# Attention start on one core: square sums split between two engines, softmax in halves, loads and conversion steps moved

## The chip, the cores and the metric

The kernel runs on one core of one Trainium2 chip. Its time is device microseconds of one execution; the number compared is the median over several runs. A profile is one further execution, taken by the hardware profiler. In what follows PE is TensorE (matmuls), PEld its weight loads, DVE is VectorE, ACT is ScalarE, POOL is GpSimd and SP is SyncE, which issues the DMAs. L12 is line 12 of the kernel.

## The reference

The attention runs over channels (256 x 256 scores, summed over 6016 tokens), then two dense blocks follow over the 6016 tokens.

```python
qn = q / (norm(q, axis=1) + 1e-6); kn = k / (norm(k, axis=1) + 1e-6)   # per channel, over tokens
s = kn.T @ qn / tau; a = softmax(s)            # 256 x 256
x = v @ a                                      # 6016 x 256
h = x @ w_in                                   # 256 -> 2048
g = where(h >= 1, h, where(h <= -1, 0, (h + 1)**2 / 4)); x = g @ w_out     # 2048 -> 256
xn = x / sqrt(mean(x*x) + 1e-6) * rms_g
out = (silu(xn @ w_gate) * (xn @ w_val)) @ w_out2                          # 256 -> 1536 -> 256
```

q, k, v and tau are float32. The five weight matrices come as float64.

## The kernel before, in words

**Start.** q and k come in 14 pieces of 2 to 4 rows per partition (`QK_CHUNKS`, 47 rows in all), one DMA each for q (L369) and k (L370), into 9 rotating tiles `qk`. For each piece ACT squares q and k (L379), DVE adds the squares into the four-row sum `acc` in SBUF (L381), and PE multiplies the raw k by the raw q: `scores(ci, b)` (L354) does the piece `ci` for the half `b` of the 256 score rows, one float32 matmul per row, which the profile shows as two matmul instructions of 256 columns each. Half 0 of a piece is written out when the piece comes, half 1 five pieces later (`BEHIND`). After the last piece DVE folds `acc` to one row (L387), PE sums it over the partitions into `n_ps` and `k_ps` (L409, L411), ACT takes the roots, DVE the reciprocals (L482 to L487), and the scaled scores go through the softmax (L491 to L497).

**First quarter of w1.** The kernel never forms v @ a: since x @ w_in = v @ (a @ w_in), it makes w1 = a @ w_in in four quarters of 512 columns, each for two halves of 128 rows. For `product_a(0)` (L441) PE first transposes both halves of the exponentials (L503), ACT and DVE split them into a high and a low part (`ah`, `al`, L126 and L123); then come 6 matmuls of 512 columns per half (L451), and ACT writes the high and DVE the low part of w1 (L460, L461). DVE and ACT work here in the order in which it is written (`in_order`).

**Float64 weights.** Each weight tile of 512 KB (`wide`, L195 and L197) is turned into a high and a low float32 part by `narrow` (L203): DVE clamps (L206), ACT or DVE takes the low word (L211, L213), DVE joins (L217, L225) and subtracts (L123), ACT takes the absolute value and the high part (L221, L231). This is cut into five steps; `pump()` (L271) takes each of up to two running jobs one step further and begins another. In the start three tiles of w_in are converted so (`PUMPS`); in the main loop there is one pump per block and another at every third. `gates` holds steps back behind given instructions.

**Main loop.** For each tile of 512 tokens and each of 16 slices of the 2048 columns, a block ("1", t, f) does six matmuls for h (`emit_A`, L553), ACT and DVE compute g (L570 to L572) and split it (L126, L123), and three blocks later six matmuls add to y (`emit_B`, L587). Tiles 0 and 1 are interleaved: (0,0), (0,1), (1,0), (0,2), ... The quarters 1 to 3 of w1 are made at blocks 5, 13 and 21 (`make_w1`). Blocks ("2", t, f) of the second dense block begin after 60 blocks of the first kind. h and the start's small products share four PSUM buffers (`mm_tile`).

**Order.** The instruction order of each engine is set ahead of time by a planner, from the order in which they are written, priorities (`AHEAD_OF`) and its own estimate of times; `in_order` fixes the written order for the engines it names. On the chip each engine works strictly through its list.

Of the kernel before, what the change touches and what calls it, by code (L numbers as in the profile page):

```python
# [34 lines left out]
BEHIND = 5  # L35
AHEAD = 3
# [13 lines left out]
def tile_channel_attention_two_ffn(  # L50
# [152 lines left out]
    def narrow(x, hi, lo, on_act):  # L203
# [26 lines left out]
        got = low.bitcast(F32)  # L230
        nc.scalar.activation(out=hi, in_=got, func=AF.Copy)  # L231
# [11 lines left out]
    def narrow_job():  # L243
        if not wide:
            fetch()
        key, x, dst = wide.pop(0)
        ahead = STAGE - FLIGHT
        if BORROW[0] <= n_wide[0] < BORROW[1]:
            ahead += LENT
        while jobs and n_wide[0] >= EARLY and len(wide) < ahead:  # L250
            fetch()
        hi, lo = dst()
        yield from narrow(x, hi, lo, key[0] != "wo")
        ready.add(key)
# [11 lines left out]
    may_W2 = [False]  # L266

# [3 lines left out]
    def pump():  # L271
        for job in flight[:]:
            if step_job(job) == "end":
                flight.remove(job)
        if len(flight) < FLIGHT and (wide or jobs) and (key_next() in FIRST or may_W2[0]):
            job = narrow_job()
            step_job(job)
            flight.append(job)

# [44 lines left out]
    for at_job, job in zip((1, 4, 5, 8, 9), late_wi):  # L324
        later.insert(at_job, job)
# [21 lines left out]
    acc = sp.tile([P, 2, JM, C], F32, name="acc")  # L347
# [16 lines left out]

    for ci, nj in enumerate(QK_CHUNKS):
# [19 lines left out]
        h = {NQ - 3: 2, NQ - 1: 1}.get(ci)  # L385
        if h:
            last_sum = nc.vector.tensor_tensor(  # L387
                out=acc[:, :, :h, :], in0=acc[:, :, :h, :], in1=acc[:, :, h:2 * h, :],
                op=ALU.add,
            )  # L390
        scores(ci, 0)
        if ci >= BEHIND:
            scores(ci - BEHIND, 1)
        if ci in FETCH_AT:
# [46 lines left out]
    def product_a(g):  # L441

        h, l = wi.pop(g)
        got = []
        for b in range(NC):
            ah, al = at[b]
            ps = mm_tile(f"w1_ps{g}_{b}")
            terms = [(ah, w, c) for c in range(NC) for w in (h, l)]
            terms += [(al, h, c) for c in range(NC)]
            for i, (x, w, c) in enumerate(terms):  # L450
                nc.tensor.matmul(  # L451
                    ps, x[:, c * P:(c + 1) * P], w[:, c, :],
                    start=(i == 0), stop=(i == len(terms) - 1),
                )
            got.append(ps)

        def evict(b):
            sl = slice(g * TOK, (g + 1) * TOK)
            hi, lo = w1h[:, b, sl], w1l[:, b, sl]
            nc.scalar.activation(out=hi, in_=got[b], func=AF.Copy, scale=rs[b])  # L460
            nc.vector.scalar_tensor_tensor(  # L461
                out=lo, in0=got[b], scalar=rs[b], in1=hi.bitcast(F32),
                op0=ALU.mult, op1=ALU.subtract,
            )
            if b == NC - 1:
                w1_made.add(g)
# [3 lines left out]
    ENG = mybir.EngineType  # L470
    with in_order(ENG.DVE, ENG.Activation):
        with tc.issue_after(last_sum.ins):
            for c in range(NC):
                turn_v(0, c)
        nc.scalar.activation(out=rq, in_=n_ps[:, :C], func=AF.Sqrt)
        nc.scalar.activation(
            out=rk, in_=k_ps[:, :2 * NC].rearrange("p (b x) -> p b x", x=2)[:, :, 0],
            func=AF.Sqrt,
        )

        nc.scalar.activation(out=seen, in_=ones[:, :1], func=AF.Exp)
        nc.vector.tensor_scalar(out=rq, in0=rq, scalar1=1e-6, scalar2=None, op0=ALU.add)  # L482
        nc.vector.reciprocal(out=rq, in_=rq)
        nc.vector.tensor_scalar(
            out=rk, in0=rk, scalar1=1e-6, scalar2=tau_sb, op0=ALU.add, op1=ALU.mult
        )
        nc.vector.reciprocal(out=rk, in_=rk)  # L487
        for c in range(NC):
            v_hi(0, c)
        for b in range(NC):  # L490
            nc.vector.scalar_tensor_tensor(  # L491
                out=s_sb[b], in0=s_ps[b], scalar=rk[:, b:b + 1], in1=rq,
                op0=ALU.mult, op1=ALU.mult,
            )
            nc.vector.tensor_reduce(out=mx[b], in_=s_sb[b], op=ALU.max, axis=AX.X, negate=True)

            nc.scalar.activation(  # L497
                out=s_sb[b], in_=s_sb[b], func=AF.Exp, bias=mx[b], accum_out=rs[b]
            )
        a_ps = [mm_tile(f"a_ps{b}")[:, :C] for b in range(NC)]  # L500
        for b in range(NC):
            for c in range(NC):
                nc.tensor.transpose(  # L503
                    a_ps[b][:, c * P:(c + 1) * P], s_sb[b][:, c * P:(c + 1) * P], ident
                )
        v_lo(0, 0)
        for b in range(NC):
            ah = atp.tile([P, C], F32R, name=f"ah{b}")
            al = atp.tile([P, C], F32R, name=f"al{b}")
            split(ah, al, a_ps[b])  # L510
            at.append((ah, al))
            nc.vector.tensor_scalar(
                out=rs[b], in0=rs[b], scalar1=1e-9, scalar2=None, op0=ALU.add
            )
            nc.vector.reciprocal(out=rs[b], in_=rs[b])
# [392 lines left out]
```

## Time and profile before

| | us |
|---|---|
| median of 3 runs | 1175.72 (1175.22 to 1175.86) |
| profiled execution | 1174.88 |
| its span in the trace | 1173.1 |
| PE busy in the span | 1156.6 (99%) |
| DVE busy | 661.6 (56%) |
| ACT busy | 642.2 (55%) |
| GpSimd busy | 69.6 (6%) |

The span is what the trace covers; 1.8 us of the execution lie around it. Busy shares are averages over the whole span. The page's slices of 29 us and the table by stretch show where an engine is full. A row of a timeline gives start, duration, engine, line, operation and tiles, and in brackets how long the engine had stood idle before it and what ended that.

### The profile page before, as it was taken

How to read it: one execution, taken by the hardware profiler on the slowest of the kernel's cores; microseconds unless marked ns; L12 is line 12 of the kernel's file. 1: busy time of each engine (PE TensorE's matmuls, PEld its weight loads, DVE VectorE, ACT ScalarE, POOL GpSimd, SP SyncE). 2: the span in 40 equal slices, each digit the busy share in tenths (PEclk: the TensorE clock that was granted, in tenths of full speed). 3: DMA queues.
4: the chain of work that ended last, by engine and by line, in shares of the span. 5: the costliest groups of instructions: out<-in, count | busy, mean ns of one | idle time of the engine just before them, and what ended most of it. 6: DMA issues, size and time to landing. Idle time of an engine off the chain costs nothing.

```text
span 1173.1 us, 14011 instructions
## 1 busy us (share of the span) xinstructions
PE 1156.6 (99%) x5202; PEld 966.7 (82%) x5202; DVE 661.6 (56%) x1034; ACT 642.2 (55%) x1092; POOL 69.6 (6%) x54
## 2 busy tenths in 40 slices
PE   8889999999999999999999999999999999999998
PEld 7768878888888888888888888888888888888898
DVE  5999999844554554553554454464454455553433
ACT  6688899755555545555554554554545454333332
POOL 0000000100100101101101100010010011010000
PEclk9999999999999999999999999999999999999999
DMA  9923344010020020010011001002001001010110
GB/s 351 233 107 100 98 116 118 1 19 1 1 36 1 1 36 1 1 28 9 1 18 18 1 12 25 1 1 32 1 1 18 1 1 19 1 18 1 19 18 14
DMA packets 107747, 43.36 MB, mean 37 GB/s; under 512 B 97568, under 2 KB 97952, under 8 KB 107680
## 3 DMA queue, kind: packets, MB, share of 16 engines
q1 hardware_dynamic: 107680, 42.48, 14.6%
q8 instruction: 40, 0.66, 0.2%
q14 instruction: 27, 0.22, 0.1%
HBM read 36.31 MB, written 6.16 MB: 36 GB/s over the span
## 4 chain that ended last, share of the span: by engine, by line
PE 87%; DVE 5%; DMA 3%; ACT 3%; SPq 1%; issue 1%; ACTq 0%; DVEq 0%
PE y L595 18%; PE h L561 18%; PE gp L675 16%; PE vp L675 16%; PE o L719 15%; DVE acc L381 1%; PE o L709 1%; DMA qk<-in_k_dram 1%; DMA wide<-in_moe_w_val_dram 1%; SPq L164 1%; DMA wide<-in_moe_w_out_dram 1%; DVE g L572 1%; ACT g L570 1%; DMA qk<-in_q_dram 1%; ACT gh L126 1%
## 5 line engine op out<-in xcount | busy, mean ns | idle before, releaser
L572 DVE SCALAR_TENSOR_TENSOR g<-h,g 128x512 f32<-128x512 f32 (+1 forms) x192 | 129.9, 677 | 157.3 <-ACT g L571 157.1
L126 ACT ACTIVATE uh<-u 128x512 fp32r<-128x512 f32 (+1 forms) x144 | 89.8, 623 | 206.2 <-PE o L719 170.7
L686 DVE TENSOR_TENSOR u<-u,vp 128x512 f32<-128x512 f32 (+1 forms) x144 | 97.2, 675 | 159.5 <-PE vp L675 156.9
L570 ACT ACTIVATE g<-h 128x512 f32<-128x512 f32 (+1 forms) x192 | 111.9, 586 | 115.6 <-PE h L561 112.6
L126 ACT ACTIVATE gh<-g 128x512 fp32r<-128x512 f32 (+1 forms) x192 | 119.0, 621 | 82.6 <-DVE g L572 82.1
L561 PE MATMUL h<-vh,w1h 128*128 128x512 f32 (+1 forms) x384 | 148.8, 388 | 2.2 <-DVE g L572 2.2
L123 DVE TENSOR_TENSOR ul<-u,uh 128x512 fp32r<-128x512 f32 (+1 forms) x144 | 97.6, 678 | 92.0 <-ACT uh L126 85.4
L561 PE MATMUL h<-vl,w1h 128*128 128x512 f32 (+1 forms) x384 | 148.8, 388 | 0.0
L595 PE MATMUL y<-gh,woh 128*128 128x512 f32 (+1 forms) x384 | 148.0, 385 | 0.8 <-ACT gh L126 0.6
L595 PE MATMUL y<-gh,wol 128*128 128x512 f32 (+1 forms) x384 | 147.7, 385 | 0.0
L123 DVE TENSOR_TENSOR gl<-g,gh 128x512 fp32r<-128x512 f32 (+1 forms) x168 | 113.6, 678 | 56.0 <-ACT gh L126 54.7
L685 ACT ACTIVATE u<-gp 128x512 f32<-128x512 f32 (+1 forms) x144 | 84.8, 589 | 79.7 <-PE gp L675 66.6
L571 ACT ACTIVATE g<-g 128x512 f32<-128x512 f32 (+1 forms) x192 | 118.6, 622 | 4.5
L561 PE MATMUL h<-vh,w1l 128*128 128x512 f32 (+1 forms) x384 | 117.9, 387 | 0.0
L595 PE MATMUL y<-gl,woh 128*128 128x512 f32 (+1 forms) x384 | 117.0, 386 | 0.7 <-DVE gl L123 0.7
L675 PE MATMUL gp<-xh,wgl 128*128 128x512 f32 (+1 forms) x288 | 111.0, 385 | 0.0
L675 PE MATMUL gp<-xh,wgh 128*128 128x512 f32 (+1 forms) x288 | 111.0, 385 | 0.0
L675 PE MATMUL vp<-xh,wvl 128*128 128x512 f32 (+1 forms) x288 | 110.9, 385 | 0.0
L675 PE MATMUL vp<-xh,wvh 128*128 128x512 f32 (+1 forms) x288 | 110.9, 385 | 0.0
L719 PE MATMUL o<-uh,wdl 128*128 128x512 f32 x264 | 102.8, 390 | 0.0
L719 PE MATMUL o<-uh,wdh 128*128 128x512 f32 x264 | 102.8, 389 | 0.0
L675 PE MATMUL gp<-xl,wgh 128*128 128x512 f32 (+1 forms) x288 | 87.6, 385 | 0.0
(121 smaller groups left out, 1731.6 us busy)
## 6 DMA issues: line engine op xcount, KB each, us to landing
wide<-in_moe_w_out_dram SPq DMA_DIRECT2D x14, 512.0 KB, 3.8
vin<-in_v_dram SPq DMA_DIRECT2D x88, 64.0 KB, 2.6
out_dram<-ob SPq DMA_DIRECT2D x88, 64.0 KB, 2.0
qk<-in_q_dram SPq DMA_DIRECT2D x9, 512.0 KB, 10.2
qk<-in_k_dram SPq DMA_DIRECT2D x9, 512.0 KB, 10.2
wide<-in_moe_w_in_dram SPq DMA_DIRECT2D x8, 512.0 KB, 5.2
wide<-in_moe_w_gate_dram SPq DMA_DIRECT2D x6, 512.0 KB, 3.5
wide<-in_moe_w_val_dram SPq DMA_DIRECT2D x6, 512.0 KB, 3.9
```

The source lines that it names most:

```text
L123: return eng.tensor_tensor(out=dst_lo, in0=src, in1=hi.bitcast(F32), op=ALU.subtract)
L126: nc.scalar.activation(out=dst_hi, in_=src, func=AF.Copy)
L164: nc.sync.dma_start(out=xv[32 * a:32 * a + 32, c, :n // 32, :], in_=src[a, c])
L561: nc.tensor.matmul(ps[:, :n], w[:, c, f * P:(f + 1) * P], x[:, c, :n], start=(i == 0), stop=(i == len(terms) - 1),)
L570: nc.scalar.activation(out=r[:, :n], in_=ps[:, :n], func=AF.Relu, bias=0.5, scale=0.5)
L571: on_act = nc.scalar.activation(out=r[:, :n], in_=r[:, :n], func=AF.Square)
L572: on_dve = nc.vector.scalar_tensor_tensor(out=r[:, :n], in0=ps[:, :n], scalar=1.0, in1=r[:, :n], op0=ALU.max, op1=ALU.min)
L595: nc.tensor.matmul(y_ps[t][:, c, :n], w[:, f, c * P:(c + 1) * P], x[:, :n], start=(f == 0 and w is woh and x is gh), stop=(f == NF1 - 1 an ...
L675: nc.tensor.matmul(ps[:, :n], w[:, c, f * P:(f + 1) * P], x[:, c, :n], start=(i == 0), stop=(i == len(terms) - 1),)
L685: nc.scalar.activation(out=u[:, :n], in_=ps[0][:, :n], func=AF.Silu)
L686: nc.vector.tensor_tensor(out=u[:, :n], in0=u[:, :n], in1=ps[1][:, :n], op=ALU.mult)
L719: nc.tensor.matmul(o_ps[t][:, c, :n], w[:, f, c * P:(c + 1) * P], x[:, :n], start=(f == 0 and w is wdh and x is uh), stop=(f == NF2 - 1 an ...
```

## The change

- q and k come in 16 pieces, (1, 1, 2, 2, 2, 4, ..., 4, 3, 2, 2). PE does the scores in the written order: half 0 of a piece when it comes, half 1 up to the piece that `SECOND_AT` names. After the last piece come half 1 of pieces 9 and 10, then the norm matmuls, then half 1 of pieces 11 to 15 (15 rows).
- The square sums are two rows wide. GpSimd adds pieces 3, 5, 7, 9 and 11 into `acc` in SBUF, DVE adds the others into two PSUM tiles `ad`, which ACT starts by squaring piece 2 into them. At the end DVE adds `ad` and `acc`; the norm matmuls run over two rows, so there are twice as many.
- The three early w_in loads are issued after pieces 3, 5 and 7 instead of 5, 6 and 7. tau and rms_g are loaded after the last q and k load instead of after the second piece. Three more weight tiles are loaded around the first v tile, ahead of the second.
- Softmax, transposes, split, product and eviction are done for half 0 and then for half 1, with PE, DVE and ACT all in written order. Three h blocks are begun with their first three matmuls (half 0 of w1) before half 1 of w1 is evicted. The gates that held conversion steps behind the preparation of v are not set there any more. `step_first` would take one running conversion a step further.
- In the main loop the extra conversion step at every third block is left out while a `task` (preparation of v, normalisation) is waiting. `AHEAD_OF` is 400 instead of 300.

```diff
-AHEAD_OF = 300
+AHEAD_OF = 400
-QK_CHUNKS = (2, 2, 4, 4, 4, 4, 4, 4, 4, 4, 4, 3, 2, 2)
-PUMPS = (0, 0, 0, 0, 0, 0, 0, 2, 2, 3, 3, 3, 2, 0)
-FETCH_AT = (5, 6, 7)
+QK_CHUNKS = (1, 1, 2, 2, 2, 4, 4, 4, 4, 4, 4, 4, 4, 3, 2, 2)
+SECOND_AT = (1, 2, 3, 4, 5, 6, 6, 7, 7, 8, 8, 8, 8, 9, 9, 9)
+SQ_BUFS = 3
+TO_PSUM = 2
+ON_POOL = (3, 5, 7, 9, 11)
+NORMS_AT = 11
+W_IN_AT = (3, 5, 7)
+PUMPS = (0, 0, 0, 0, 0, 1, 1, 2, 2, 2, 2, 2, 3, 0, 0, 0)
+FETCHED = 5
...
+    def step_first():
+        if flight and step_job(flight[0]) == "end":
+            del flight[0]
...
-    for at_job, job in zip((1, 4, 5, 8, 9), late_wi):
+    for at_job, job in zip((0, 3, 4, 7, 8), late_wi, strict=True):
...
+    products = ExitStack()
+    products.enter_context(in_order(ENG.PE))
...
-        if ci == 1:
-            nc.sync.dma_start(out=tau_sb, in_=tau.broadcast_to([P, 1]))
-            nc.sync.dma_start(out=rg, in_=rms_g.rearrange("(c p) -> p c", p=P))
...
-        if not first:
-            last_sum = nc.vector.tensor_tensor(
-                out=acc[:, :, :nj, :], in0=acc[:, :, :nj, :], in1=sq, op=ALU.add
-            )
+            if ci in ON_POOL:
+                for r in range(0, nj, JS):
+                    nc.gpsimd.tensor_tensor(
+                        out=acc, in0=acc, in1=sq[:, :, r:r + JS, :], op=ALU.add
+                    )
+            elif not first:
+                for r in range(nj):
+                    nc.vector.tensor_tensor(
+                        out=ad[r % JS], in0=ad[r % JS], in1=sq[:, :, r, :], op=ALU.add
+                    )
         scores(ci, 0)
-        if ci >= BEHIND:
-            scores(ci - BEHIND, 1)
+        for cj in range(SECOND_AT[ci - 1] if ci else 0, SECOND_AT[ci]):
+            scores(cj, 1)
...
     while flight:
         pump()
+    pumped[0] = True
     with tc.issue_after(last_load.ins):
+        nc.sync.dma_start(out=tau_sb, in_=tau.broadcast_to([P, 1]))
+        fetch()
         load_v(0)
+        fetch()
+        fetch()
         load_v(1, lent=True)
+        nc.sync.dma_start(out=rg, in_=rms_g.rearrange("(c p) -> p c", p=P))
...
+    softmax(0)
+    step_first()
+    turn_a(0)
+    step_first()
+    evict = product_a(0, 0)
+    softmax(1)
+    evict()
+    v_lo(0, 0)
+    turn_a(1)
+    evict = product_a(0, 1)
+    v_lo(0, 1)
+    for f in range(BEGUN):
+        begun[0, f] = emit_A(0, f)
+        next(begun[0, f])
+    turn_v(1, 0)
+    evict()
...
-    gates += [on_act.ins, on_dve.ins]
...
-        if i % 3 == 0:
+        if i % 3 == 0 and not tasks:
             pump()
```

## Rows read from the trace of the kernel before

**Rows 1.** The page: its first line, the span and all instructions.

```profile
span 1173.1 us, 14011 instructions
```

**Rows 2.** Table by stretch: PE, PEld, DVE, ACT, POOL busy (instructions), PE clock, DMA share, GB/s.

```profile
20.00:40.00 20.00, 20.00 (x94) 17.65 (x93) 19.48 (x18) 16.86 (x21) 0.00 (x0) 1.00 1.06 382
...
80.00:100.00 20.00, 20.00 (x90) 16.56 (x89) 19.63 (x36) 17.84 (x33) 0.00 (x0) 1.00 0.31 84
```

**Rows 3.** Timeline of PE, scores to w1's second quarter.

```profile
4.57 42.09 PE L357 MATMUL s_ps<-qk 128*128 128x256 f32 x180 [4.57 <-DMA qk<-in_k_dram]
46.87 0.67 PE L409 MATMUL n_ps<-acc,ones 128*128 128x256 f32 x2 [0.22 <-DVE acc L387]
47.74 1.97 PE L357 MATMUL s_ps<-qk 128*128 128x256 f32 x8
52.14 0.41 PE L503 MATMUL a_ps<-ident,s_sb 128*128 128x128 f32 x2 [2.43 <-ACT s_sb L497]
52.90 0.44 PE L503 MATMUL a_ps<-ident,s_sb 128*128 128x128 f32 x2 [0.35 <-ACT s_sb L497]
53.16 1.19 PE L451 MATMUL w_ps<-wi,ah 128*128 128x512 f32 x4
...
56.02 0.39 PE L561 MATMUL h<-vh,w1h 128*128 128x512 f32 x1
...
64.02 0.50 PE L561 MATMUL h<-vh,w1h 128*128 128x512 f32 x1 [2.24 <-DVE g L572]
...
68.47 0.39 PE L451 MATMUL w_ps<-w1h,ah 128*128 128x512 f32 x1
...
71.71 0.50 PE L451 MATMUL w_ps<-w1l,ah 128*128 128x512 f32 x1 [0.95 <-DVE w1l L123]
```

**Rows 4.** Table by stretch, same columns: the stretch in which PE's clock fell.

```profile
66.00:68.00 2.00, 2.00 (x6) 1.55 (x5) 2.00 (x4) 2.00 (x5) 0.00 (x0) 0.50 0.00 0
```

**Rows 5.** Timeline of DVE: after the roots, then the first blocks.

```profile
47.99 0.29 DVE L482 TENSOR_SCALAR rq<-rq 128x256 f32<-128x256 f32 x1
...
61.40 0.43 DVE L206 TENSOR_SCALAR wide<-wide 128x512 f32<-128x512 f32 x1 [1.36 <-DMA wide<-in_moe_w_out_dram]
...
63.28 1.29 DVE L572 SCALAR_TENSOR_TENSOR g<-h,g 128x512 f32<-128x512 f32 x2
```

**Rows 6.** Timeline of ACT: squares as pieces land, then half 0's exponential and split.

```profile
6.69 0.63 ACT L379 ACTIVATE acc<-qk 128x512 f32<-128x512 f32 x1 [0.15 <-DMA qk<-in_k_dram]
9.61 1.06 ACT L379 ACTIVATE sq<-qk 128x1024 f32<-128x1024 f32 x1 [2.29 <-DMA qk<-in_q_dram]
10.90 1.06 ACT L379 ACTIVATE sq<-qk 128x1024 f32<-128x1024 f32 x1 [0.23 <-DMA qk<-in_k_dram]
...
30.33 1.06 ACT L379 ACTIVATE sq<-qk 128x1024 f32<-128x1024 f32 x1 [0.16 <-DMA qk<-in_k_dram]
...
51.40 0.51 ACT L497 ACTIVATE s_sb<-s_sb,mx 128x256 f32<-128x256 f32 x1 [0.76 <-DVE mx L495]
...
52.75 0.36 ACT L126 ACTIVATE ah<-a_ps 128x256 fp32r<-128x256 f32 x1
```

**Rows 7.** Groups of instructions on GpSimd by shape: busy us, mean ns.

```profile
L123 POOL TENSOR_TENSOR gl<-g,gh 128x512 fp32r<-128x512 f32 x21 | 27.0, 1286 | 410.1 <-ACT gh L126 410.1
L123 POOL TENSOR_TENSOR gl<-g,gh 128x384 fp32r<-128x384 f32 x3 | 3.0, 1016 | 58.9 <-ACT gh L126 58.9
```

**Rows 8.** Timeline of SP: the v loads and a late weight load.

```profile
34.16 12.25 SPq L164 DMA_DIRECT2D vin<-in_v_dram  x16
...
57.25 0.49 SPq L197 DMA_DIRECT2D wide<-in_moe_w_out_dram  x1
```

**Rows 9.** Timeline of PE, 160 to 215 us: its idle times.

```profile
166.57 0.50 PE L595 MATMUL y<-gh,woh 128*128 128x512 f32 x1 [0.63 <-ACT gh L126]
168.04 0.73 PE L595 MATMUL y<-gl,woh 128*128 128x512 f32 x2 [0.26 <-DVE gl L123]
206.86 0.74 PE L595 MATMUL y<-gl,woh 128*128 128x512 f32 x2 [0.40 <-DVE gl L123]
```

More of the change, by code (lines that the diff above doesn't have):

```diff
@@ L24 @@
 PE_FROM = 32
+BEGUN = 3
 GATED = 50
 PACE = 1
-AHEAD_OF = 300
+AHEAD_OF = 400
 BLAG = 3
@@ L249, in narrow_job @@
             ahead += LENT
-        while jobs and n_wide[0] >= EARLY and len(wide) < ahead:
+        while jobs and n_wide[0] >= FETCHED and len(wide) < ahead:
             fetch()
-        hi, lo = dst()
-        yield from narrow(x, hi, lo, key[0] != "wo")
+        yield from narrow(x, dst, key[0] != "wo")
         ready.add(key)
@@ L274, in pump @@
                 flight.remove(job)
-        if len(flight) < FLIGHT and (wide or jobs) and (key_next() in FIRST or may_W2[0]):
+        if len(flight) < FLIGHT and (wide or jobs and pumped[0]) and (key_next() in FIRST or may_W2[0]):
             job = narrow_job()
@@ L439, in tile_channel_attention_two_ffn, with product_a, evict @@
     w1_made = set()
[L441 to L457, printed above, removed]
+    def product_a(g, b):
+        h, l = wi[g]
+        ah, al = at[b]
+        ps = mm_tile(f"w1_ps{g}_{b}")
+        terms = [(ah, w, c) for c in range(NC) for w in (h, l)]
+        terms += [(al, h, c) for c in range(NC)]
+        for i, (x, w, c) in enumerate(terms):
+            nc.tensor.matmul(
+                ps, x[:, c * P:(c + 1) * P], w[:, c, :],
+                start=(i == 0), stop=(i == len(terms) - 1),
+            )
+        def evict():
@@ L468, in product_a, with emit_A @@
-        return evict
[L470 to L475, printed above, removed]
+            w1_made.add((g, b))
+        return evict
+    def emit_A(t, f):
+        _, n = tiles[t]
+        vh, vl = v_op[t]
+        ps = mm_tile(f"h{t}_{f}")
+        for c in range(NC):
+            assert (f * P // TOK, c) in w1_made
+            for i, (w, x) in enumerate(((w1h, vh), (w1h, vl), (w1l, vh))):
+                nc.tensor.matmul(
+                    ps[:, :n], w[:, c, f * P:(f + 1) * P], x[:, c, :n],
+                    start=(c == 0 and i == 0), stop=(c == NC - 1 and i == 2),
+                )
+            yield ps
@@ L500, in tile_channel_attention_two_ffn @@
[L500 to L515, printed above, removed]
@@ new lines, in tile_channel_attention_two_ffn @@
+    products.close()
+    products.enter_context(in_order(ENG.PE, ENG.DVE, ENG.Activation))
+    with tc.issue_after(last_sum.ins):
+        turn_v(0, 0)
+    turn_v(0, 1)
+    nc.scalar.activation(out=rq, in_=n_ps[:, :C], func=AF.Sqrt)
+    nc.scalar.activation(
+        out=rk, in_=k_ps[:, :2 * NC].rearrange("p (b x) -> p b x", x=2)[:, :, 0],
+        func=AF.Sqrt,
+    )
+    nc.scalar.activation(out=seen, in_=ones[:, :1], func=AF.Exp)
+    nc.vector.tensor_scalar(out=rq, in0=rq, scalar1=1e-6, scalar2=None, op0=ALU.add)
@@ new lines, in tile_channel_attention_two_ffn @@
+    nc.vector.reciprocal(out=rq, in_=rq)
+    nc.vector.tensor_scalar(
+        out=rk, in0=rk, scalar1=1e-6, scalar2=tau_sb, op0=ALU.add, op1=ALU.mult
+    )
+    nc.vector.reciprocal(out=rk, in_=rk)
+    for c in range(NC):
+        v_hi(0, c)
+    softmax(0)
[9 more added lines that the diff above has]
+    v_lo(0, 1)
+    begun = {}
+    for f in range(BEGUN):
+        begun[0, f] = emit_A(0, f)
+        next(begun[0, f])
@@ L529, in tile_channel_attention_two_ffn @@
+    turn_v(1, 0)
+    evict()
+    v_hi(1, 0)
+    turn_v(1, 1)
+    v_lo(1, 0)
+    v_hi(1, 1)
+    v_lo(1, 1)
+    products.close()
     start.close()
@@ L543, in make_w1 @@
         require(*[("wi", g, c) for c in range(NC)])
-        evict = product_a(g)
-        evicts.extend((evict, b) for b in range(NC))
+        evicts.extend(product_a(g, b) for b in range(NC))
     y_ps = {}
@@ L788, in step1 @@
     def step1(t, f):
-        ps = emit_A(t, f)
+        for ps in begun.pop((t, f), None) or emit_A(t, f):
+            pass
         m1.append((t, f))
@@ L824, in did_D @@
             store(t)
-    jobs.extend(later)
     ordered = ExitStack()
```

133 lines of the change are left out of this document (59 added, 74 removed).

## Prediction

> **What bounds the kernel now.** I read the page first: its span is 1173.1 us [rows 1], PE is busy in 99% of it, no other engine in more than 56%. PE's matmuls are the same before and after but for six more small ones, so the change can win only where PE stands idle or runs slowly, and the table by stretch says where that is. From 80 to 100 us and in the stretches after it PE is full, 90 matmuls in 20 us; from 20 to 40 us it is full too, with 94 of the scores' matmuls [rows 2], which is 0.2128 us each. The idle time is at the start, so the timelines come next.
>
> PE works from 4.57 us to 46.66 on the scores without a gap, waits 0.22 for the sums, and finishes the scores at 49.71. Then it waits 2.43 and 0.35 for the two exponentials, starts the product at 53.16 and the first h at 56.02, stops 2.24 before 64.02 because DVE computes g late, and 0.95 before 71.71 [rows 3]. In between its clock is granted at 0.50, the lower of its two levels (1.2 of 2.4 GHz) [rows 4]: the twelve matmuls from 64.02 to 68.47 take 4.45 us instead of 12 x 0.227 = 2.72, a loss of 1.73. The clock fell after the second long gap, not after the first. DVE was late because it stood 1.36 us before a clamp for a weight tile and then had conversion steps ahead of g at 63.28 [rows 5].
>
> So before, the start loses 4.57 + 0.22 + 2.78 + 2.24 + 1.73 + 0.95 = 12.5 us on PE. All terms below are made against the profiled execution, 1174.88 us, of which 1173.1 are span; the runs' median is 0.84 us above it, and I add that at the end.
>
> **1. Scores: PE gets a new wait, +2.65.** Smaller first pieces let PE start some 0.8 us earlier. But the written order gives PE only half 0 of most pieces and keeps half 1 of pieces 9 to 15 for the end. When piece 12 is due, PE has 36 rows of half 0 and 20 of half 1 behind it, 112 matmuls. Before, its first 180 took 42.09 [rows 3] where 180 x 0.2128 makes 38.3, so the first ones cost 3.8 more. Starting at 3.8 it is through 112 at 3.8 + 3.8 + 112 x 0.2128 = 31.4. Piece 12 brings row 40. Before, the last k of row 32 (with the three w_in tiles, as in the change) landed at 30.33, and a DMA of 512 KB takes 1.28 us (9.61 to 10.90) [rows 6]: row 40, four DMAs on, is there at 35.45. Taking tau and rms_g off the queue saves at most 2.92 - 1.28 = 1.64 (6.69 to 9.61 for one 512 KB DMA [rows 6]), and the small pieces (four more DMAs in all) eat some of it; I take 1.0 of the bounds 0 and 1.64. So piece 12 comes at 34.45, and PE will have waited some 3 us. After it come 76 matmuls (16.17) and twelve norm matmuls at the price of six from 46.87 to 47.74, twice 0.87 [rows 3]: scores end at 34.45 + 16.17 + 1.74 = 52.36 instead of 49.71. Bounds: 53.4 if nothing is saved, 49.8 if PE never waits (0.8 earlier, 0.87 more).
>
> The sums then don't matter much. GpSimd has no row of 1024 elements; its adds of 512 and 384 take 1.286 and 1.016 [rows 7], so 1.286 + 512 x 0.0021 = 2.37 each, nine of them 21.3 us, beside the loads. The bounds are 1.29 (as one of 512) and 2.57 (two). DVE does 25 rows of 512 into PSUM; the nearest rows, g from PSUM, go two in 1.29 us [rows 5], so some 15 us, bounds 11 (0.43 each, as the clamp in the same rows) and 17 (0.69 each, if none overlaps: the 1.29 are 0.60 and 0.69). The last piece lands near 39; two squares, two adds and two final adds make the sums ready near 42.3. PE comes to the norms 30 matmuls and 1.74 before 52.36, at 44.2, so 1.9 us of cover is left. From the norm's start to the end of the first exponential it was 5.04 us (46.87 to 51.91 [rows 3, 6]), 0.9 more with twice the matmuls: 50.2, which the 30 matmuls hide. The v tile could use up that cover: sixteen v loads take 12.25 us to issue [rows 8] and come behind a weight tile now; if tile 0 lands at 46, DVE transposes until 47.3 and the exponential ends some 3.9 us later (47.99 to 51.91), at 51.2. Still hidden, by 1.1.
>
> **2. Softmax and product in halves, -0.45.** Before, from the last score to the first h it was 6.31 us [rows 3]. After, PE transposes half 0 at once. Its product starts 0.82 later (ACT's split 0.36 and the ways between [rows 6]) and takes 1.36. Half 1 can't be scaled before DVE has done half 0's low part and reciprocal (about 1.5 after the last score); scale, maximum and exponential bring the second transposes to 3.1, with 0.9 idle on PE. ACT evicts half 0 of w1 before it splits half 1: product at 4.0. Its last two matmuls wait for the low part, which stands on DVE behind that eviction and `v_lo(0,0)`, until 5.4: first h at 5.85, with 2.35 idle in all. So the halves exchange one gap for four. The begun blocks (9 matmuls, 2.05) hide half 1's eviction. Bounds -1.0 (the low part not late) and +1.5 (the exponential not hidden).
>
> **3. First blocks, -4.65.** Three weight tiles come ahead of the second v tile instead of behind or among v (one was issued at 57.25 [rows 8]), so the 1.36 us on DVE goes. Without the gates their steps may stand in DVE's gaps before the blocks, some 7 us of DVE work, and g is no longer behind them. I take 0.27 of the 2.24 + 1.73 + 0.95 = 4.92 as left. Bounds: all stays (0), all goes (-4.92). If DVE is late again, PE's clock may fall again: 1.73 of it.
>
> **4. Fewer steps, other priorities, -0.8.** PE idles 0.63 + 0.26 + 0.40 = 1.29 between 166 and 207 us for split parts of g [rows 9]. By the loop's own count five extra steps go (blocks 18, 21, 36, 48, 51) and the conversions end three blocks later, at block 51; the second dense block begins after 60, so nothing new waits. Bounds -1.29 and +1.29, since the order of everything there is planned anew.
>
> `step_first` does nothing: `while flight: pump()` has emptied the list before. Cost zero.
>
> Sum: 2.65 - 0.45 - 4.65 - 0.8 = -3.25, so 1171.6 for the profile and 1172.5 for the median.
>
> **A rule that speaks against it.** The trace shows GpSimd's adds only while DVE is not working on two SBUF operands, so no row here shows what they do to each other. The Trainium skill, page "SBUF — State Buffer", section "SBUF: two separate sides", says that a DVE instruction with two SBUF inputs and a GpSimd instruction that reads SBUF take turns: the later one is blocked until the other has ended. By it the sum would be that of rival C; without it, the sum above.
>
> **Rivals.**
>
> A. Forecast, -3.25; its own range -5 to -1.5.
>
> B. PE hardly waits for the pieces: scores end at 50.4 or before, so -3.25 - 2 = -5.3 or more, 1170.4. For it: the start of the queue is uneven before (1.3 us per 512 KB later on, 2.9 once), so small pieces may gain more than I grant. Against it: 12 MB must come before piece 12, at a pace that no edit changes.
>
> C. Slower: in the start GpSimd adds are on for 21 of some 28 us, and the twelve conversion steps of the three w_in tiles that read two SBUF operands or clamp wait on DVE for the running add. From about 12 us on DVE has 15 + 6.7 (three times 0.43 + 3 x 0.6) + 1.2 = 22.9 us of work; with a wait of w each the sums are ready at 34.9 + 12 w. Above w = 0.8 PE waits at the norms, above 1.05 the gain is gone. With 1.5, two thirds of an add, the norms start at 52.9 instead of 44.2, and the time is -3.25 + 8.7 = +5.4: 1181.2. For it: GpSimd is on nearly all the time. Against it: the adds into PSUM have one SBUF operand and run on, and some steps will meet no add.
>
> D. It does not do what it says: the planner leaves the conversion steps behind the products, DVE is as full in the first blocks as in 80 to 100 us (19.63 of 20 [rows 2]), and only the DMA's 1.36 goes. 2.65 - 0.45 - 1.36 - 0.8 = 0: 1175.8. For it: all of these steps are written behind the products. Against it: DVE stands idle some microseconds there.
>
> **How the numbers follow.** A 0.42, B 0.16, D 0.24, C 0.18. A measurement of this kernel can tell 0.2%, 2.4 us. A is beyond that in 8 of 10, B always, D is within it in two thirds and slower in the rest, C is slower in 8 of 10: faster 0.50, same 0.27, slower 0.23. The range takes A and D whole, B down to 1168.5 and C's mild part up to 1178: 1168.5 to 1178.
>
> **What would show it.** Step 1: waits of PE for q and k pieces between 12 and 35 us, some 3 us in all, and the last score near 52.4. Step 2: four gaps of half to one us in the 6 us after it. Step 3: no wait for g and no clock at 0.50 between 58 and 75 us, conversion steps on DVE before the first h. Step 4: less than 1.3 us idle from 160 to 210. The prediction is wrong if PE has no waits before 35 us (B), if the norms wait for the sums with conversion steps stretched beside GpSimd's adds (C), or if g is late again (D).

## The result, and the profile after

The change makes the kernel 0.9% slower: 1186.68 us (median of 4 runs, 1185.84 to 1186.98) against 1175.52 before on the same chip; ratio 1.0094, 95% interval 1.0076 to 1.0111. The profiled execution took 1185.84 us, its span is 1183.9, 10.8 over before [rows 1]. The prediction, 1172.5 with a range to 1178, was wrong in sign and size.

The timeline of PE after, scores to the first h (start, duration, work, idle time ahead of it and what ended that; for [rows 3]):

```profile
35.96 10.42 PE L373 MATMUL s_ps<-qk 128*128 128x256 f32 x46 [0.52 <-DMA qk<-in_k_dram]
53.73 2.04 PE L442 MATMUL n_ps<-acc,ones 128*128 128x256 f32 x4 [7.35 <-ACT wide L227]
55.57 1.70 PE L447 MATMUL k_ps<-ones,acc 128*128 128x2 f32 x8
57.13 8.49 PE L373 MATMUL s_ps<-qk 128*128 128x256 f32 x30
65.46 0.38 PE L528 MATMUL a_ps<-ident,s_sb 128*128 128x128 f32 x2
66.32 1.21 PE L484 MATMUL w_ps<-wi,ah 128*128 128x512 f32 x4 [0.47 <-ACT ah L132]
...
71.36 0.39 PE L508 MATMUL h<-vh,w1h 128*128 128x512 f32 x1
```

PE stands 7.35 us ahead of the norms, then works them and the last 30 scores slowly; the first h starts at 71.36 instead of 56.02. From there to the end of the span it is 1112.5 us, before 1117.1. So the change loses 15.3 us ahead of the first h and wins 4.5 behind it.

The releaser named at the norms, a conversion step of ACT, had nothing to do with the sums. What they waited for is on DVE, in its timeline after:

```profile
11.47 1.49 DVE L212 TENSOR_SCALAR wide<-wide 128x512 f32<-128x512 f32 x1 [10.11 <-DMA wide<-in_moe_w_in_dram]
13.07 0.69 DVE L223 SCALAR_TENSOR_TENSOR wide<-wide 128x512 uint32<-128x512 uint32 x1
...
18.41 2.45 DVE L223 SCALAR_TENSOR_TENSOR wide<-wide 128x512 uint32<-128x512 uint32 x1 [1.06 <-ACT wide L217]
21.60 2.04 DVE L231 SCALAR_TENSOR_TENSOR wide<-wide 128x512 uint32<-128x512 uint32 x1 [0.74 <-ACT wide L227]
...
27.72 2.24 DVE L212 TENSOR_SCALAR wide<-wide 128x512 f32<-128x512 f32 x1
30.07 2.65 DVE L223 SCALAR_TENSOR_TENSOR wide<-wide 128x512 uint32<-128x512 uint32 x1
...
39.69 2.49 DVE L411 TENSOR_TENSOR ad<-ad,sq 128x512 f32<-128x512 f32 x4 [1.29 <-ACT sq L403]
44.78 6.08 DVE L411 TENSOR_TENSOR ad<-ad,sq 128x512 f32<-128x512 f32 x10 [2.60 <-ACT sq L403]
...
52.30 0.68 DVE L223 SCALAR_TENSOR_TENSOR wide<-wide 128x512 uint32<-128x512 uint32 x1
52.90 0.68 DVE L438 TENSOR_TENSOR acc<-ad,acc 128x512 f32<-128x512 f32 x1
```

and in the timeline of GpSimd after:

```profile
10.32 2.36 POOL L406 TENSOR_TENSOR acc<-acc,sq 128x1024 f32<-128x1024 f32 x1 [9.03 <-ACT sq L403]
17.95 5.13 POOL L406 TENSOR_TENSOR acc<-acc,sq 128x1024 f32<-128x1024 f32 x2 [5.27 <-ACT sq L403]
27.32 4.85 POOL L406 TENSOR_TENSOR acc<-acc,sq 128x1024 f32<-128x1024 f32 x2 [4.24 <-ACT sq L403]
37.91 9.69 POOL L406 TENSOR_TENSOR acc<-acc,sq 128x1024 f32<-128x1024 f32 x4 [5.74 <-ACT sq L403]
```

A clamp (L212) takes 0.42 us alone and a combining step (L223, L231) 0.69. The five that meet a GpSimd add take 1.49 to 2.65, and they end soon after that add: the two clamps 0.28 behind it, the three steps 0.55. The step of 21.60 ends at 23.64, 0.56 after GpSimd's pair (17.95 + 5.13 = 23.08); that of 30.07 at 32.72, 0.55 after the next pair. The profile shows the wait as a longer instruction, not as idle time. The five are 7.96 us longer than alone. DVE's adds into PSUM, which read SBUF once, keep their 0.6 us a row beside GpSimd (39.69, 44.78).

Who waits for these steps is in the waits of ACT from 8 to 56 us (in total, times, longest):

```profile
ACT wide L227 <- DVE wide L223: 11.2, 4, 5.0
ACT sq L403 <- POOL acc L406: 2.6, 2, 1.4
```

and in its timeline:

```profile
20.89 0.67 ACT L227 ACTIVATE wide<-wide 128x512 f32<-128x512 f32 x1 [2.52 <-DVE wide L223]
...
32.75 0.67 ACT L227 ACTIVATE wide<-wide 128x512 f32<-128x512 f32 x1 [5.00 <-DVE wide L223]
33.32 1.04 ACT L403 ACTIVATE sq<-qk 128x1024 f32<-128x1024 f32 x1
...
47.63 2.19 ACT L403 ACTIVATE sq<-qk 128x512 f32<-128x512 f32 x4 [1.41 <-POOL acc L406]
...
53.02 0.66 ACT L227 ACTIVATE wide<-wide 128x512 f32<-128x512 f32 x1 [2.65 <-DVE wide L223]
```

L227 is the next step of the same weight tile, and in ACT's queue the squares stand behind it. While ACT waited 5.00 us for the step of 30.07, no square was made; pieces that had landed reached GpSimd and DVE late, GpSimd worked until 47.60, and twice ACT waited for a buffer of squares that GpSimd held. Of the 11.2 us, the last 2.65 came when all squares were made, so some 8.5 held squares up; in the run without GpSimd below (e1) the same waits are 1.0 up to there. The last sum was ready at 53.58. Last, the clock (table by stretch, columns as in [rows 2]):

```profile
46.00:50.00 4.00, 0.38 (x2) 0.00 (x0) 4.00 (x8) 2.59 (x6) 1.59 (x1) 1.00 1.12 304
50.00:52.00 2.00, 0.00 (x0) 0.00 (x0) 2.00 (x5) 0.37 (x1) 0.00 (x0) 0.62 1.20 131
52.00:60.00 8.00, 6.27 (x19) 5.39 (x20) 7.64 (x15) 3.71 (x8) 0.00 (x0) 0.50 0.65 133
60.00:62.00 2.00, 2.00 (x9) 1.68 (x8) 0.07 (x1) 1.08 (x4) 0.00 (x0) 0.82 0.79 198
```

In the long wait the granted clock fell to 0.50, its lower level. Norms and 30 scores took 65.46 - 53.73 = 11.73 us; the forecast had 1.74 + 6.38 = 8.12 for them, so 3.6 are lost to the clock.

### The profile page after: what moved, and what is told of

Its sections match the earlier page's. It is cut to its first block, busy times and chain, and to the rows that moved or that the text cites. A ratio compares the mean times of both kernels' runs of the same rounds, so it can differ in the third digit from the quotient of the medians.

```text
span 1183.9 us, 14056 instructions
## 1 busy us (share of the span) xinstructions
PE 1160.4 (98%) x5208; PEld 968.1 (82%) x5208; DVE 659.8 (56%) x1047; ACT 641.1 (54%) x1098; POOL 91.5 (8%) x63
## 4 chain that ended last, share of the span: by engine, by line
PE 87%; DVE 5%; DMA 5%; ACT 1%; SPq 1%; issue 1%; POOL 0%; ACTq 0%
PE y L635 18%; PE h L508 18%; PE gp L715 16%; PE vp L715 16%; PE o L759 15%; DMA qk<-in_k_dram 2%; PE o L749 1%; DVE g L612 1%; DVE gl L129 1%; DMA qk<-in_q_dram 1%; PE w_ps L484 1%; SPq L170 1%; PE s_ps L373 1%; DVE wide L231 1%; DMA wide<-in_moe_w_in_dram 1%
## 5 line engine op out<-in xcount | busy, mean ns | idle before, releaser
L129 DVE TENSOR_TENSOR ul<-u,uh 128x512 fp32r<-128x512 f32 (+1 forms) x144 | 97.6, 678 | 91.7 <-ACT uh L132 85.1
L508 PE MATMUL h<-vh,w1l 128*128 128x512 f32 (+1 forms) x384 | 147.4, 385 | 0.0
L129 DVE TENSOR_TENSOR gl<-g,gh 128x512 fp32r<-128x512 f32 (+1 forms) x168 | 113.1, 676 | 56.1 <-ACT gh L132 54.8
```

Of the source, the lines that this page charges most:

```text
L129: return eng.tensor_tensor(out=dst_lo, in0=src, in1=hi.bitcast(F32), op=ALU.subtract)
L508: nc.tensor.matmul(ps[:, :n], w[:, c, f * P:(f + 1) * P], x[:, c, :n], start=(c == 0 and i == 0), stop=(c == NC - 1 and i == 2),)
```

## Experiments

The theory: GpSimd's adds stop DVE's conversion steps, ACT's squares queue behind these, the sums come late, PE waits and loses its clock. All times in us; "norms", "transposes" and "first h" are the starts of these matmuls, "rest" is the span less the start of the first h. These four are read from one profiled execution, which lay up to 1.9 us from the median of its row (e4h: 1177.50). The runs were made on several chips, and each ratio is to the kernel before on the same chip (medians 1174.36 to 1175.52).

| Run | norms | transposes | first h | rest | median | ratio to before, interval |
|---|---|---|---|---|---|---|
| before | 46.87 | 52.14 | 56.02 | 1117.1 | 1175.52 | 1 |
| after | 53.73 | 65.46 | 71.36 | 1112.5 | 1186.68 | 1.0094 (1.0076 to 1.0111) |
| e1, no GpSimd | 46.96 | 55.26 | 61.17 | 1113.0 | 1176.00 | 1.0012 (1.0002 to 1.0021) |
| e2, conversions late | 46.84 | 58.56 | 66.93 | 1114.0 | 1182.04 | 1.0061 (1.0044 to 1.0077) |
| e3, norms last | 53.29 | 61.37 | 69.25 | 1114.0 | 1185.29 | 1.0088 (1.0073 to 1.0103) |
| e5, idle adds | 49.49 | 57.80 | 63.70 | 1113.2 | 1180.25 | 1.0044 (1.0029 to 1.0060) |
| e6, adds by rows | 49.05 | 60.70 | 66.61 | 1113.0 | 1181.21 | 1.0050 (1.0035 to 1.0065) |
| e4, old start | 47.20 | 54.60 | 62.44 | 1116.7 | 1180.83 | 1.0049 (1.0034 to 1.0064) |
| e4g, held to 2nd exponential | 46.47 | 51.74 | 59.12 | 1115.4 | 1176.28 | 1.0008 (0.9998 to 1.0017) |
| e4h, held to the end | 46.79 | 52.06 | 58.67 | 1116.7 | 1175.61 | 1.0012 (1.0002 to 1.0022) |
| b2, earlier scores | 45.76 | 55.75 | 63.10 | 1113.6 | 1178.70 | 1.0030 (1.0018 to 1.0043) |
| b3, one late piece | 45.06 | 51.64 | 57.54 | 1114.8 | 1174.53 | 0.9999 (0.9989 to 1.0008) |
| b4, same, not held | 45.78 | 54.00 | 59.97 | 1113.2 | 1174.82 | 1.0000 (0.9990 to 1.0009) |
| b5, held to 1st exponential | 45.66 | 52.45 | 59.54 | 1113.3 | 1174.25 | 0.9999 (0.9990 to 1.0007) |
| b6, same, no GpSimd | 45.60 | 52.18 | 58.69 | 1113.5 | 1174.87 | 0.9999 (0.9991 to 1.0008) |
| e7a, old pieces | 52.98 | 58.61 | 64.53 | 1116.4 | 1183.65 | 1.0077 (1.0060 to 1.0095) |
| e7b, old, one late | 52.24 | 57.78 | 63.74 | 1116.2 | 1180.75 | 1.0049 (1.0034 to 1.0064) |

**e1: no sums on GpSimd.**

```diff
-ON_POOL = (3, 5, 7, 9, 11)
+ON_POOL = ()
```

> All square sums on VectorE into PSUM, none on GpSimd; everything else of the change stays. Theory (GpSimd's adds stop VectorE's conversion steps, ScalarE's squares queue behind them): no conversion step over 0.8 us, GpSimd has no work in the first 60 us, the norms' first product at 46 to 48 instead of 53.73 us, the clock full at 60 us, the first product of h at 60 to 63 instead of 71.36 us, the time 1174 to 1178. Rival 1 (it is the amount of adding, VectorE's now 43 rows at 0.6 us): the norms at 52 or later, the time 1184 or more. Rival 2 (the small first pieces and the scores' order starve TensorE, whoever adds): the norms earlier, but the last score still at 64 to 66 and the time 1182 or more.

All of the theory's numbers came. PE in this run:

```profile
35.90 10.39 PE L373 MATMUL s_ps<-qk 128*128 128x256 f32 x46 [0.56 <-DMA qk<-in_k_dram]
46.96 1.10 PE L442 MATMUL n_ps<-acc,ones 128*128 128x256 f32 x4 [0.67 <-ACT wide L227]
```

DVE does all 43 rows itself and is ready 6.8 us sooner than with help. Taking GpSimd out wins back 9.7 of the 10.8 us of span (1174.2). What is left is of the kind that rival 2 named, but far smaller: PE still waits for pieces, and the first transposes start at 55.26, behind the last score, not at 64 to 66.

**e2: GpSimd keeps its adds, the conversions go behind them.** The conversion steps are moved behind sums and norms:

```diff
-PUMPS = (0, 0, 0, 0, 0, 1, 1, 2, 2, 2, 2, 2, 3, 0, 0, 0)
+PUMPS = (0,) * 16
...
+    gates[:] = [last_sq.ins, last_sum.ins]
+    for _ in range(15):
+        pump()
     while flight:
         pump()
+    gates.clear()
```

> GpSimd keeps its five pieces; the early conversions of the weight tiles are written behind the sums and the norms, so that none runs beside a GpSimd add. Theory: squares go through without a stop over 0.5 us on ScalarE, GpSimd's adds end before 44 us instead of 47.60, the norms' first product at 44 to 48 us. The conversions then stand between norms and first product and cost some 8 us there (12 steps of 0.66): first h at 60 to 64, the time 1175 to 1180. Rival 1 (the adds themselves and the buffers of squares that they hold are too slow): the norms at 51 or later in spite of it, the time 1188 or more, since the conversions come on top.

GpSimd's adds take the same time (timeline of GpSimd, its last piece):

```profile
34.34 4.80 POOL L406 TENSOR_TENSOR acc<-acc,sq 128x1024 f32<-128x1024 f32 x2 [0.32 <-ACT sq L403]
```

It is through at 39.14 instead of 47.60, and the norms start at 46.84: rival 1 falls. The time missed (1182.04, not 1175 to 1180), and so did the first h (66.93, not 60 to 64): with the conversions in the softmax chain PE stood 3.25 ahead of the transposes, and its clock was 0.59 from 60 to 70 us.

**e5: nine adds that nobody reads,** in e1.

```diff
+    idle = opp.tile([P, NC, TOK], F32, tag="op", name="idle")
+    nc.gpsimd.memset(idle, 0.0)
+    for _ in range(9):
+        nc.gpsimd.tensor_tensor(out=idle, in0=idle, in1=idle, op=ALU.add)
```

> The version with all square sums on VectorE, and beside it nine GpSimd adds of 128x1024 in SBUF on a tile that nobody reads, one behind the other from the start (some 21 us). Theory (the adds block VectorE's conversion steps whatever they add): most conversion steps between 11 and 26 us take 1.4 us or more instead of 0.42 to 0.71, VectorE's adds into PSUM stay at 0.6 us a row, the norms come at 49 to 53 instead of 46.96 us, the time is 1178 to 1184 against 1176.0 without the idle adds. Rival (the loss came from sums that passed through GpSimd and the square buffers that it held): within 1 us of 1176.0.

The timelines of GpSimd and of DVE in this run:

```profile
2.11 18.71 POOL L387 TENSOR_TENSOR idle<-idle 128x1024 f32<-128x1024 f32 x9
```

```profile
12.29 2.18 DVE L223 SCALAR_TENSOR_TENSOR wide<-wide 128x512 uint32<-128x512 uint32 x1
14.39 1.28 DVE L415 TENSOR_TENSOR ad<-ad,sq 128x512 f32<-128x512 f32 x2
...
17.53 1.54 DVE L129 TENSOR_TENSOR wi<-wide,wi 128x512 fp32r<-128x512 f32 x1 [0.75 <-ACT wi L238]
```

Work on data that is in nobody's chain moves the norms by 2.5 us, the span by 2.7 (1176.9) and the median by some 4. Five steps, clamps and the L129 above included, are stretched, by 3.5 us in sum; only two of them pass 1.4 us, where I had expected most. From 20.8 us on, when the adds are through, no step is stretched.

**e6: the same bytes in twice as many instructions,** in the changed kernel.

```diff
+                    for j in range(JS):
                         nc.gpsimd.tensor_tensor(
-                            out=acc, in0=acc, in1=sq[:, :, r:r + JS, :], op=ALU.add
+                            out=acc[:, :, j, :], in0=acc[:, :, j, :],
+                            in1=sq[:, :, r + j, :], op=ALU.add
```

> The changed kernel with each GpSimd add of 128x1024 cut into two of 128x512, the same bytes. Theory (VectorE gets its turn when the running GpSimd instruction ends): GpSimd adds of about 1.2 us, no conversion step longer than about 1.9 us (0.69 and a wait of at most 1.2), the norms at 49 to 52 instead of 53.73, the time 1179 to 1184. Rival (VectorE waits until GpSimd's queue is empty, or the loss is the adding itself): steps of over 2 us stay, the time 1186 or more.

The longest step was 1.57 us instead of 2.65:

```profile
26.10 1.57 DVE L223 SCALAR_TENSOR_TENSOR wide<-wide 128x512 uint32<-128x512 uint32 x1
```

The norms came at 49.05 and the time is some 5 us better than after, as the theory has it: the wait ends with the running instruction. GpSimd's own adds got longer where they met conversion steps. Its timeline:

```profile
17.22 6.37 POOL L407 TENSOR_TENSOR acc<-acc,sq 128x512 f32<-128x512 f32 x4 [4.72 <-ACT sq L403]
...
33.07 9.89 POOL L407 TENSOR_TENSOR acc<-acc,sq 128x512 f32<-128x512 f32 x8 [2.56 <-ACT sq L403]
```

Beside DVE's adds into PSUM (33.07) an add takes 1.24; among the conversion steps (17.22) the mean is 1.59, and the single adds behind a stopped step take up to 1.74. So the two engines take turns, and GpSimd waits as well. Two pairs of runs have the same adds on DVE and differ on GpSimd: from e1 to e5 the steps are stretched by 3.5 us and the norms come 2.5 later (46.96, 49.49); from e6 to after the stretch goes from some 4 to 8 us and the norms from 49.05 to 53.73.

**e3: all scores ahead of the norms.**

```diff
-NORMS_AT = 11
+NORMS_AT = 16
```

> The norms' products stand behind all scores in TensorE's order instead of ahead of the last 30; nothing else is changed. Theory: the sums are as late as in the changed kernel (norms at 53 to 54 us), but TensorE fills its wait with the 30 scores (6.4 us at full clock), so the idle 7.35 us shrinks to about 1, the clock does not fall there or falls a little; the softmax chain, about 8 us from norms to first transpose, is then covered by nothing: first h at 65 to 67 instead of 71.36, the time 1180 to 1183. Rival: the sums are late because TensorE or its buffers hold them up: the norms move too, and the time stays within 1 us of 1186.7.

PE's wait at the norms shrank to 0.73 with the norms where they were, so PE did not delay the sums. But the wait came back as 6.20 ahead of the transposes, and there the clock fell (0.50 from 60 us): 1185.29, less won than the theory had, close to the rival's number for another reason. Idle time moved is not idle time removed.

**e4, e4g, e4h: the old start with the later steps of the change.** Pieces, sums in SBUF and order of scores as before; loads, halves, begun blocks and fewer steps as after. In e4g and e4h the later tiles' conversion steps are held back; the line

```diff
-    softmax(1)
+    exp_1 = softmax(1)
...
+    gates[:] = exp_1
```

is e4g's (softmax returns its maximum and its exponential), and e4h's

```diff
-    v_hi(1, 1)
-    v_lo(1, 1)
+    on_act = v_hi(1, 1)
+    on_dve = v_lo(1, 1)
+    gates[:] = [on_act.ins, on_dve.ins]
```

> The start of the kernel before (its 14 pieces, square sums in SBUF on VectorE, its order of scores and norms) with the rest of the change: loads late, softmax and product by halves, three blocks begun, no gates there, fewer conversion steps. Theory (all the loss is in the first step, the other steps gain as forecast): first h at 51 to 53 us instead of 56.02 before, the time 1170 to 1173. Rival 3 (halves, begun blocks or the lost gates cost as well): 1175 or more.

> The old start with the later steps of the change once more, but the later weight tiles' conversion steps held back until the second half's maximum and exponential. Theory (it was these steps in the softmax chain that cost 2.5 us and then the clock, not the halves): first transposes at 52 to 53 instead of 54.60 us, the clock full until the first product of h, that product at 57.5 to 59 instead of 62.44, the time 1170 to 1174. Rival (halves and begun blocks cost as they stand): first h at 60.5 or later and 1177 or more.

> The old start with the later steps of the change, and the later conversion steps held back, as in the kernel before, until the last step of v's second tile. Theory (the halves and begun blocks are worth what was forecast once no conversion step stands in them): first transposes at 51.5 to 52.3, transposes to first h 5.8 to 6.2 us at full clock (7.6 with the conversions let in behind the exponential), first h at 57.3 to 58.4, the time 1171.5 to 1174. Rival (what is held back is then late for the blocks): longer waits for the converted output weights than the 1.12 us of the run before, the time 1175 or more.

All three missed their times. In e4 conversion steps stood between the roots and the first half's exponential, PE waited 4.55 and its clock was at 0.50 from 54 to 64 us: rival 3. Holding them back gave the transposes as expected or better (51.74, 52.06). In e4g the steps let in behind the second exponential then stretched transposes to first h to 7.38; in e4h the first blocks wait. PE in e4h:

```profile
52.06 0.41 PE L514 MATMUL a_ps<-ident,s_sb 128*128 128x128 f32 x2 [2.43 <-ACT s_sb L507]
52.95 1.79 PE L470 MATMUL w_ps<-wi,ah 128*128 128x512 f32 x4 [0.47 <-ACT ah L134]
...
65.23 0.50 PE L494 MATMUL h<-vh,w1h 128*128 128x512 f32 x1 [0.91 <-DVE g L599]
...
70.62 0.79 PE L470 MATMUL w_ps<-w1h,ah 128*128 128x512 f32 x1 [2.34 <-DVE g L599]
```

The wait for g, 2.24 before [rows 3], is there again as 2.34: what step 3 wins hangs on conversion steps ahead of the first blocks. In e4 and e4g this wait is 0.67, as after, and step 3's gain is there: counted from the first h, the first 300 matmuls take 71.4 and 71.5 us (before 73.9, after 70.6). Their rest is long further on, where PE waits for split parts of g: the next 400 take 95.7 and 94.6 us (before 93.5, after 92.7). Why, no run shows.

**b2: e1 with more second halves early,** and the steps held as in e4g.

```diff
-SECOND_AT = (1, 2, 3, 4, 5, 6, 6, 7, 7, 8, 8, 8, 8, 9, 9, 9)
+SECOND_AT = (1, 2, 3, 4, 5, 6, 7, 8, 8, 9, 10, 10, 10, 11, 11, 11)
```

> All square sums on VectorE; the second halves of the scores earlier in TensorE's order, so that it waits less for data between 12 and 36 us; conversion steps held out of the softmax chain as in the run with the old start. Theory (without GpSimd the rest of the loss is TensorE's waits for q and k, 0.6 us five times): waits between 12 and 36 us under 1 us in sum, last score at 51 to 52.5 instead of 55.26, first transposes right behind it, first h at 57 to 58.5 instead of 61.17, the time 1170 to 1173. Rival (the norms and the chain behind them, not the scores, set the first transposes): first transposes at 53 or later, time 1174 or more.

PE waited 0.95 and 0.59 for pieces and then ran 126 matmuls without a gap; but it came to the norms early:

```profile
45.76 1.10 PE L442 MATMUL n_ps<-acc,ones 128*128 128x256 f32 x4 [2.48 <-DVE acc L438]
47.50 8.41 PE L373 MATMUL s_ps<-qk 128*128 128x256 f32 x30
```

After 2.48 us of waiting the clock was at 0.50 from 48 to 50 us, and the last 30 scores took 8.25 instead of 6.5. The steps let in behind the second exponential stretched transposes to h to 7.35. The rival's time.

**b3: one late piece on GpSimd, 22 products behind the norms,** SECOND_AT as in b2, steps held as in e4h.

```diff
-ON_POOL = (3, 5, 7, 9, 11)
-NORMS_AT = 11
+ON_POOL = (11,)
+NORMS_AT = 12
```

> The changed kernel with its own pieces, GpSimd on the twelfth piece alone, the second halves of the scores earlier, 22 score products behind the norms, later conversion steps held back as before. Theory: no step over 0.8 us, the norms at 43.5 to 45.5, TensorE without a wait of over 0.5 us between 16 and 50 us and with its full clock, last score and first transposes at 51.5 to 53, first h at 57.4 to 59, the time 1170 to 1173. Rival (sums are late again, TensorE runs dry before the norms and loses its clock, as with the same order and no GpSimd): a wait of over 1.5 us ahead of the norms, the time 1176 or more.

The mechanism came as forecast, step for step, transposes at 51.64 and first h at 57.54; the time did not (1174.53, no change), since the rest is 1114.8: the held steps make g late again (2.39 ahead of w1's second quarter).

**e7a, e7b: 14 old pieces with sums in PSUM,** e7a without GpSimd, e7b with it on one piece.

```diff
-SECOND_AT = (1, 2, 3, 4, 5, 6, 6, 7, 7, 8, 8, 8, 8, 9, 9, 9)
+SECOND_AT = (0, 0, 0, 0, 0, 1, 2, 3, 4, 5, 6, 7, 8, 9)
```

> The changed kernel with the 14 pieces and the order of the scores of the kernel before, all square sums on VectorE into PSUM, later conversion steps held back as before. Theory: no waits of TensorE between 12 and 40 us, no stretched steps, the norms at 46.5 to 48, first transposes at 52 to 54, first h at 58 to 60, the time 1172 to 1176. Rival (sums by rows in PSUM are slower than the old 128x2048 adds by more than the 0.03 us a row): norms after 48.5, the time 1177 or more.

> As the kernel with the old pieces and sums in PSUM, but GpSimd adds one piece, the eleventh, which comes when the early conversions are nearly through; these start one piece sooner, and 14 instead of 8 score products stand behind the norms. Theory (GpSimd's add costs VectorE nothing where no conversion step meets it): at most two stretched steps, VectorE's last sum some 2 us sooner, the norms at 44 to 45.5, first transposes at 49.5 to 51, first h at 55.5 to 57, the time 1168 to 1172, under the kernel before. Rival (GpSimd's 4.8 us for a piece hold a buffer of squares, or meet a conversion step, and the last sums wait for it): norms after 46.5, the time 1174 or more.

Both missed, by the design of the runs: the changed kernel writes PE's order out, and this order keeps no second half for the early waits (1.56, 0.33, 1.65 and 1.01 in e7a). The norms waited for PE (52.98), not for the sums, which were ready at 45.81 and, with one late piece on GpSimd, at 44.03: that much of the theory held.

**b4, b5, b6: which holding is worth what.** Open was why b3 gains nothing. b4 is b3 with the steps not held, b5 holds them to the first half's maximum and exponential, b6 is b5 with `ON_POOL = ()`.

> GpSimd on the twelfth piece alone, second halves of the scores earlier, 22 score products behind the norms, later conversion steps not held back. Theory (these steps stand in sums and softmax chain and cost there 0.8 to 2 us, but nothing is late behind): the norms at 45 to 46, first transposes at 52.2 to 53.5 instead of 51.64, transposes to first h 5.9, no wait of 2.39 us behind the blocks, the time 1172 to 1174.5 beside some 1174.9 for the kernel before. Rival (the steps hide in VectorE's idle times): transposes at 51.6 to 52, the time 1170 to 1172.

> The same, but the later conversion steps are held back until the first half's maximum and exponential. Theory: norms at 45, first transposes at 51.6 to 52, steps in VectorE's idle time behind the maximum, transposes to first h 5.9 to 6.6, the longest wait behind the blocks about 1.2 us, the time 1171 to 1173.5, the quickest of these versions. Rival (they land in the second half's chain as they did behind the second exponential): transposes to first h 7.3 or more, the time 1174 or more.

> The same with all sums on VectorE. Theory (the one late piece takes 2.4 us of VectorE's adds off its last stretch, but the scores set the end): sums some 1 to 1.5 us later than with the piece on GpSimd, TensorE waits 0.5 to 1.2 us ahead of the norms, the time 0.5 to 1.5 us over the run with it. Rival (GpSimd's add costs as much as it saves): equal within 0.4 us.

Not held, they put the transposes at 54.00, a little more than expected, and the rest at 1113.2. Held to the first exponential they stretch the second half's chain (its transposes wait 1.47 us) and the rest is the same. Held to the end they leave the chain alone and lengthen the rest to 1114.8. First h and rest trade against each other: b3 to b6 have spans of 1172.2 to 1173.2, and none differs from the kernel before by more than the measurement is uncertain. The late piece on GpSimd shows no gain: the last sum is ready at 45.51 with it (b5) and at 45.44 without (b6), and the medians, 0.62 apart, are closer than the intervals can tell. No version was found that beats the kernel before.

## Why the prediction was wrong

**Step 1 failed, at "The sums then don't matter much".** The forecast had them ready near 42.3; they were ready at 53.58. The single costs were sized well (a GpSimd add 2.40 in the mean against 2.37, DVE's adds into PSUM 0.6 a row as assumed); what failed is the overlap, which let GpSimd's adds and DVE's conversion steps run side by side. Of the first h's 13.15 us over its forecast (71.36 against 52.36 + 5.85), 7.35 is PE's wait for the sums and 3.6 the clock behind it; 1.5 is piece 12, which came at 35.96 and not at 34.45, and 0.6 is that the 46 matmuls after it took 10.42 and not 46 x 0.2128. The waits for the pieces themselves were sized well: between 12 and 36 us in e1 0.66 + 0.60 + 0.59 + 0.58 + 0.56 = 3.0, "some 3".

**Rival C named the mechanism and mis-sized it.** Its own sign came: the norms waited for the sums, with conversion steps stretched beside GpSimd's adds. It added the waits to DVE's own work, 34.9 + 12 w, and needed w = 0.8 before PE waits. Measured, w was 7.96 / 12 = 0.66; by the formula the sums would have been in time at 42.9. Missing was the second queue: a stopped step of DVE holds the next step of its tile on ACT, and ACT's squares, whose work is DVE's and GpSimd's input, stand behind that (some 8.5 us of waits). Missing, too, was the price of PE's wait, half as much again in lost clock. Both arguments against it, on which its chance of 0.18 rested, were true and did not help: the adds into PSUM ran on, and 7 of 12 steps met no add.

For these adds the rule that the prediction set against the trace is borne out. The Trainium skill, page "SBUF — State Buffer", section "SBUF: two separate sides", has a DVE instruction with two SBUF inputs and a GpSimd instruction that reads SBUF block each other for a whole instruction. e5 and e6 agree, with steps of up to 2.18 beside adds of 1.89 to 2.22 us that nobody reads, and 1.57 where the adds are half as long; and GpSimd waits too, with single adds of 2.36 and 2.70 after. Not every row agrees: before, a longer GpSimd instruction held up no such step (last section).

**Step 2 was right where its cover held.** Transposes to first h took 5.90 (after), 5.91 (e1) and 5.90 (b3), forecast 5.85, with the gaps that were named. With the clock down it is 6.61 to 8.37 (e4h, e4, e2).

**Steps 3 and 4 were nearly right together:** the rest is 4.54 shorter, forecast 5.45. Step 3 came in part, 3.1 of 4.65: the wait for g is 0.67 instead of 2.24, the 0.95 for w1l and the 1.73 of the lower clock are gone, but 1.16 for the output weights at 82.25 is new. Waits of PE after, from 74 to 240 us (in total, times, longest):

```profile
PE y L635 <- DVE wol L129: 1.2, 1, 1.2
PE y L635 <- DVE gl L129: 0.8, 2, 0.5
PE h L508 <- DVE g L612: 0.7, 1, 0.7
PE y L635 <- ACT gh L132: 0.3, 1, 0.3
```

Step 4 won little of the idle time it named: 1.06 us of waits for split parts of g stand between 218 and 233 us where 1.29 stood before [rows 9]. Still, counted by matmuls, 3.2 us of the rest are won in the first 300 behind the first h and 1.2 later, more than step 4's 0.8; most of that lies in the slower matmuls around such waits. That step 3's gain is kept where the conversion steps come before the blocks and lost where they are held to the end (e4h, b3), and that they then cost time ahead of the first h, the prediction did not see: it added steps up that depend on each other.

Still open: why b3 to b6 all come out level with before. The rows show the trade, not that it must be even.

## What to carry to other kernels

Before giving work to GpSimd, list what VectorE does beside it with two SBUF operands or in a clamp, and follow each such step to the next engine: the price is not the wait alone but everything that stands behind the step that waits for it, in every queue that is worked off in order. Where adds must run on both engines, let VectorE's go into PSUM and keep GpSimd's away from the conversions in time. Work that is moved out of one wait has to be followed to where it then stands; in b3 to b6 what was won behind the first h was paid for ahead of it.

## What the runs showed of the hardware

- A stopped VectorE instruction shows as a longer one, with no idle time and no releaser: a 128x512 step of 0.69 us took up to 2.65 beside GpSimd adds of 128x1024. A clamp with one tensor operand, 0.42 alone, took up to 2.24. Adds with one operand in PSUM were not stretched (0.6 us a row).
- GpSimd's adds wait in turn: alone 2.36 us for 128x1024 and 1.27 for 128x512, right behind a stopped VectorE step up to 2.70 (after) and 1.74 (e6).
- Not every GpSimd instruction stops such a step. Before, a power of 128x16 ran 2.92 us, and a VectorE step with two SBUF operands inside that time took its usual 0.68. Timelines of GpSimd and of DVE before:

```profile
212.63 2.92 POOL L638 TENSOR_TENSOR m<-m,half 128x16 f32<-128x16 f32 x1
```

```profile
213.61 0.68 DVE L123 TENSOR_TENSOR gl<-g,gh 128x512 fp32r<-128x512 f32 x1
```

- TensorE's clock: after a wait of 2.43 us behind the scores it stayed full before, and fell in e4h, where 1.12 us of waiting stood some 3 us earlier; waits of 2.48 (b2), 3.12 (e6) and 7.35 us (after) were each followed or accompanied by a fall to 0.50, one of 2.00 (e5) not.
